# Attention with a 64-key window and a tanh-shrink MLP in one kernel: the first three batches and two chunks issued from one list, batch 0's V transposed on TensorE, weights loaded first

## The chip, the cores and the metric

One core of a Trainium2 chip runs the kernel. Its time is in device microseconds (us). Engines: PE (TensorE; PEld is its weight load), DVE (VectorE), ACT (ScalarE), POOL (GpSimd) and SP (SyncE). DMAs are issued by SP, ACT and POOL. An engine carries out its instructions in the order in which the program issues them.

## The reference

```python
# q, k, v: (batch 8, heads 8, seq 576, head_dim 64), float32
scores = np.matmul(q, k.transpose(0, 1, 3, 2)) / np.sqrt(D)
rel = pos[:, None] - pos[None, :]
mask = (rel >= 0) & (rel < 64)            # each query sees itself and 63 keys before it
attn = softmax(np.where(mask, scores, -1e9))
x = np.matmul(attn, v).transpose(0, 2, 1, 3).reshape(4608, 512)
h = x @ w_in                              # 512 x 2048
g = h - np.tanh(h)
out = g @ w_out                           # 2048 x 512
```

## The kernel before

Work on attention is by pairs of heads: pair g belongs to batch g // 4, four pairs to a batch, 32 in all. A pair's q and k are loaded and cast to bf16, transposed on PE with the heads' dimension on partitions (`tr_heads` for batch 0, `tr_rows` for pairs 4 to 9, `tr` for later ones), and copied from PSUM to `qs` or `qT` and `kT`. The keys are cut into nine windows of 128 (64 of them shared with the window before), the queries into nine blocks of 64. For each window PE makes the scores, ACT the exponential into `PT`, and either DVE multiplies with a 0/1 mask, or PE first writes large negative numbers where a key is hidden (`hides`), so that no mask is needed. PV multiplies with the V windows `vw`, of which there are two buffers, one for even and one for odd batches. V has a column of ones, so that the sum for the norm comes with it; DVE takes the reciprocal and multiplies (`norm`) into `xs`. PE transposes `xs` and a copy brings it to `xT`, the input of the MLP.

V gets to its windows through SBUF: a batch is loaded (`load_v`, `vall`), cast to `vb` (`cast_v`), written to every second window by five DMAs (`windows_v` and `keys_v`, called by `even_windows`), and the other windows are copied from their neighbours by DVE (`odd_windows`, L454 and L456 in the profile).

The MLP goes over nine chunks of 512 tokens. Chunk c has 16 steps h, each of four matmuls of 512 columns (`hp_mm`, L383), a tanh on ACT (L388) and a subtraction on DVE (`g_sub`, L395); and 16 steps y of four matmuls (`yp_mm`, L407), with a copy and a store after each four (`y_out`).

The order is written by hand. Batch 0's attention is issued straight through, then a loop over steps h = 0, 1, ... issues at each step one `OPS` entry (h or y of some chunk) and then whatever `at(h, fn, ...)` has put there. Chunk 0's h stand at the even steps 0 to 30, chunk 1's at 32 to 62, and chunk 0's y at 64 to 79; chunk 2 begins at step 80. Batches 1 and 2 are put between by tables of steps. From batch 3 on, the tables `STEPS`, `LOADS`, `TURNS` and `VALUES` do this.

Most loads stand in POOL's queue, in this order: batch 0's v, pairs 1 to 3, the window DMAs of batch 0, the first half of w_in, batch 1's v, pairs 4 and 5, the second half of w_in, pairs 6 and 7, the windows of batch 1, batch 2's v, pairs 8 to 11, the windows of batch 2, both halves of w_out, batch 3. An instruction in that queue that waits for a semaphore holds up all behind it.

Of the kernel before, what the change touches and what calls it, by code (L numbers as in the profile page):

```python
# [15 lines left out]
def kernel(  # L16
# [62 lines left out]
    stage, rows, whole = {}, {}, {}  # L79

# [98 lines left out]
    def load_w_in(i):  # L179
        nc.gpsimd.dma_start(out=w_in_sb[i], in_=w_in_r[:, :, 1024 * i:1024 * i + 1024])  # L180
# [39 lines left out]
    nc.vector.memset(vw[0][0:64, 0], 0.0)  # L220
# [13 lines left out]

    def tr_heads(g, which, bank, eng):

        src = stage.pop((g, which))
        tp = ps[:, bank, :].bitcast(BF16)[:, 0:E * P].rearrange("c (e p) -> c e p", e=E)
        for e in range(E):
            for h in range(2):  # L240
                nc.tensor.transpose(tp[64 * h:64 * h + 64, e, :], src[:, h, D * e:D * e + D], ident[:P, :P])
        o = qs[g % 2] if which == "q" else kT[g % NK][:, 64:]
        move(eng, o.rearrange("c (p e) -> c p e", e=E), tp.rearrange("c e p -> c p e"))
# [20 lines left out]
    def tr_rows(g, which, bank, eng):  # L264

        src = rows.pop((g, which)).rearrange("p e h d -> p e (h d)")
        tp = ps[:, bank, :].bitcast(BF16)[:, 0:E * P].rearrange("c (e p) -> c e p", e=E)
        for e in range(E):
            nc.tensor.transpose(tp[:, e, :], src[:, e, :], ident[:P, :P])
        o = qs[g % 2] if which == "q" else kT[g % NK][:, 64:]  # L270
        move(eng, o.rearrange("c (p e) -> c p e", e=E), tp.rearrange("c e p -> c p e"))

# [5 lines left out]

    def tile_scores(g, grp, banks, how="hide"):

        j0, n = GROUPS[grp]
        if how == "hide":
            hides(grp, banks)
        for i in range(n):
            j = j0 + i
            for h in range(2):
                r = slice(64 * h, 64 * h + 64)
                nc.tensor.matmul(ps[:, banks[h], 64 * i:64 * i + 64], kT[g % NK][r, 64 * j:64 * j + 128],  # L288
                                 qs[g % 2][r, 64 * j:64 * j + 64], start=how == "mask", stop=how == "mask" or i == n - 1)
        o = PT[g % NPT][:, j0:j0 + n].rearrange("p j (h t) -> p h j t", h=2)  # L290
        nc.scalar.activation(o, pair_of(banks)[:, :, 0:64 * n].rearrange("p h (j t) -> p h j t", t=64),  # L291
                             ACT.Exp, scale=scale)
        if how == "mask":
            p = PT[g % NPT][:, j0:j0 + n].rearrange("p j (h t) -> p (j h) t", h=2)
            nc.vector.tensor_tensor(p, p, mask_sb.unsqueeze(1).to_broadcast([128, 2 * n, 64]), ALU.mult)

    def tile_pv(g, banks):

        b, pr = divmod(g, NP)
        for i in range(NJ + 1):  # L300
            j = min(i, NJ - 1)
            o = 65 * (i % 5)
            for h in range(2):
                nc.tensor.matmul(ps[64 * h:64 * h + 64, banks[i // 5], o:o + 65], PT[g % NPT][:, j, 64 * h:64 * h + 64],
                                 vw[b % 2][:, j, 2 * pr + h, :], start=True, stop=True)
        ov = pair_of(banks)[:, :, 0:325].rearrange("p n (i c) -> p n i c", c=D + 1)
        rc = sm_pool.tile([128, 2, 5, 1], F32, tag="rc2", name="rc2")
        nc.vector.reciprocal(rc, ov[:, :, :, D:D + 1])
        xo = xs[b % 2].rearrange("p (n i) r d -> p n i r d", i=5)
        nc.vector.tensor_tensor(xo[:, :, :, pr, :], ov[:, :, :, 0:D], rc.to_broadcast([128, 2, 5, 64]), ALU.mult)  # L310
# [61 lines left out]
    H0_BANKS = 0, 1, 2, 3, 0, 1, 0, 1, 0, 1, 2, 0, 1, 2, 0, 1  # L372

    def hp_bank(c, m):
        return H0_BANKS[m] if c == 0 else (m + 2) % 3 if c == 1 else m % 2

    def hp_mm(c, ms, split):
# [8 lines left out]
        for m, hp in zip(ms, outs):  # L386
            th = sm_pool.tile([128, TOK], F32, tag="th", name="th")
            nc.scalar.activation(th, hp, ACT.Tanh)  # L388
            HID[c, m] = hp, th

    def g_sub(c, m):
        hp, th = HID.pop((c, m))
        if m == 0:
            gT[c] = g_pool.tile([128, M, TOK], BF16, tag="gT", name="gT")
        nc.vector.tensor_tensor(gT[c][:, m, :], hp, th, ALU.subtract)  # L395

    def yp_bank(c, s):
        if c == 0:
            return s % 2
        return (0, 2)[s % 2] if c == NC - 1 else 2  # L400
# [9 lines left out]
    def y_out(c, s):  # L410
        ysb = sm_pool.tile([128, d_model], F32, tag="ysb", name="ysb")
# [18 lines left out]
    for m in range(M):  # L430
        OPS[2 * m] = "h", 0, m
        OPS[32 + 2 * m] = "h", 1, m
        OPS[64 + m] = "y", 0, m
# [33 lines left out]
    for pr in range(NP):  # L467
        load_v(0, pr)
# [5 lines left out]
    for g in 2, 3:  # L474
        load(g, "k", G)
        load(g, "q", G)
# [212 lines left out]
```

## Time and profile before

| what | value |
|---|---|
| median of 3 runs (lowest to highest) | 334.32 us (333.44 to 335.68) |
| profiled execution: its own time / its span | 334.17 us / 332.4 us |
| PE, DVE, ACT, POOL busy in the span | 315.9, 199.5, 185.1, 110.5 us |
| L383 (h), L407 (y): matmuls of 512 columns | 576 and 560, mean 379 ns each |
| L395 subtraction on DVE, L388 tanh on ACT | mean 689 and 599 ns |
| copies from PSUM of 128x576, ACT / DVE | mean 654 / 754 ns |
| casts of 96x768 (q or k), ACT / DVE / POOL | about 830 / 370 / 830 ns |
| casts of V, 72x1024, DVE / POOL | mean 429 / 1052 ns |
| norm: reciprocal and product of 128x640 on DVE | mean 215 and 824 ns |
| exponential of 128x640 / 128x512 on ACT | mean 702 / 595 ns |
| DMA issue on POOL: load of a pair / window | about 660 / 590 ns |
| w_in's first half: issued / landed | 12.2 / 25.1 us |
| w_out's halves landed | 64.2 and 69.8 us |
| first matmul of chunk 0 / of chunk 2 | 25.1 / 89.5 us |

The profile is of one execution. Its groups of instructions give the mean duration of one; an engine's busy time is the sum of these with overlaps taken once. Matmuls are pipelined, so their mean duration is longer than the distance from one's start to the next's. The chain of waits goes back from the last instruction to what released it, and tells which engine or DMA set the time in each stretch.

### The profile page before, as it was taken

How to read it: one execution, taken by the hardware profiler on the slowest of the kernel's cores; microseconds unless marked ns; L12 is line 12 of the kernel's file. 1: busy time of each engine (PE TensorE's matmuls, PEld its weight loads, DVE VectorE, ACT ScalarE, POOL GpSimd, SP SyncE). 2: the span in 40 equal slices, each digit the busy share in tenths (PEclk: the TensorE clock that was granted, in tenths of full speed). 3: DMA queues.
4: the chain of work that ended last, by engine and by line, in shares of the span. 5: the costliest groups of instructions: out<-in, count | busy, mean ns of one | idle time of the engine just before them, and what ended most of it. 6: DMA issues, size and time to landing. Idle time of an engine off the chain costs nothing.

```text
span 332.4 us, 6239 instructions
## 1 busy us (share of the span) xinstructions
PE 315.9 (95%) x2435; PEld 175.3 (53%) x2435; DVE 199.5 (60%) x342; ACT 185.1 (56%) x339; POOL 110.5 (33%) x163
## 2 busy tenths in 40 slices
PE   6868999899999999999999999999999999999995
PEld 2544565555555655555555555555554444444444
DVE  4578698983257675767676666766665444334400
ACT  3545878872566666656666666555544344444411
POOL 8827597005920845434624493300000000000000
PEclk9599999999999999999999999999999999999999
DMA  8999998993796299384976968978004001000021
GB/s 159 184 173 191 212 161 120 199 190 101 123 198 125 41 163 236 81 118 116 176 133 113 180 142 140 204 126 205 32 34 104 32 34 63 32 34 32 32 97 64
DMA packets 46766, 40.68 MB, mean 122 GB/s; under 512 B 18416, under 2 KB 40048, under 8 KB 46544
## 3 DMA queue, kind: packets, MB, share of 16 engines
q0 software_dynamic: 21344, 20.06, 40.1%
q1 hardware_dynamic: 25184, 19.92, 23.6%
q8 instruction: 19, 0.31, 0.4%
q10 hardware_dynamic: 208, 0.29, 0.3%
q14 instruction: 11, 0.09, 0.1%
HBM read 36.70 MB, written 10.62 MB: 142 GB/s over the span
## 4 chain that ended last, share of the span: by engine, by line
PE 71%; DMA 9%; POOL 7%; DVE 7%; ACT 3%; issue 2%; POOLq 0%; DVEq 0%; ACTq 0%
PE ps L407 34%; PE ps L383 27%; DMA wi<-in_moe_w_in_dram 4%; PE ps L332 3%; DMA kall<-in_k_dram 3%; PE ps L316 3%; DVE xs L343 2%; PE ps L249 2%; DMA vw<-vb 2%; DVE qt L85 2%; POOL qall L96 1%; DVE gT L395 1%; POOL kall L96 1%; POOL vall L143 1%; POOL vb L85 1%
## 5 line engine op out<-in xcount | busy, mean ns | idle before, releaser
L383 PE MATMUL ps<-xT,wi 128*128 128x512 bf16 x576 | 146.8, 379 | 2.9 <-DVE gT L395 1.2
L407 PE MATMUL ps<-w_out_sb,gT 128*128 128x512 bf16 x560 | 140.8, 379 | 0.3 <-ACT ysb L412 0.3
L395 DVE TENSOR_TENSOR gT<-ps,th 128x512 bf16<-128x512 f32 x144 | 98.5, 689 | 68.6 <-ACT th L388 67.2
L388 ACT ACTIVATE th<-ps 128x512 f32<-128x512 f32 x144 | 86.0, 599 | 80.8 <-PE ps L383 77.0
L383 PEld LDWEIGHTS <-wi 128*128 128x128 bf16 x576 | 60.5, 113 | 48.1 <-issue 3.0
L407 PEld LDWEIGHTS <-gT 128*128 128x128 bf16 x560 | 52.2, 98 | 53.0 <-issue 0.8
L318 ACT ACTIVATE pt<-ps 128x384 bf16<-128x384 f32 x66 | 32.3, 489 | 24.1 <-PE ps L316 24.1
L85 POOL COPY vb<-vall 72x1024 bf16<-72x1024 bf16 x24 | 24.7, 1052 | 32.6 <-DMA vall<-in_v_dram 29.8
L343 DVE TENSOR_TENSOR xs<-ps,rc 64x576 bf16<-64x576 f32 x44 | 33.2, 755 | 1.1
L412 ACT ACTIVATE ysb<-ps 128x512 f32<-128x512 f32 x35 | 21.0, 599 | 18.9 <-PE ps L407 18.8
L85 DVE COPY qt<-ps 64x576 bf16<-64x576 bf16 x18 | 13.7, 760 | 24.1 <-ACT qt L83 24.1
L85 POOL COPY qb<-qall 96x768 bf16<-96x768 bf16 x20 | 16.6, 830 | 24.6 <-DVE pt L322 16.4
L332 PEld LDWEIGHTS <-pt 128*128 128x128 bf16 x198 | 16.5, 98 | 15.3 <-DVE pt L322 0.8
L332 PE MATMUL ps<-vw,pt 128*128 128x130 bf16 x198 | 22.0, 220 | 0.4 <-DVE pt L322 0.4
L316 PE MATMUL ps<-qt,kt 128*128 128x128 bf16 x198 | 21.8, 219 | 0.0
L316 PEld LDWEIGHTS <-kt 128*128 128x128 bf16 x198 | 15.4, 98 | 8.9 <-issue 0.3
L85 POOL COPY kb<-kall 96x768 bf16<-96x768 bf16 x20 | 16.6, 828 | 3.0 <-DMA kall<-in_k_dram 3.0
L322 DVE TENSOR_TENSOR pt<-pt,ps 128x1152 bf16<-128x1152 bf16 x22 | 16.4, 745 | 0.8 <-ACT pt L318 0.8
L83 ACT ACTIVATE kt<-ps 128x576 bf16<-128x576 bf16 x22 | 14.4, 654 | 1.6 <-PE ps L249 1.5
L291 ACT ACTIVATE pt<-ps 128x640 bf16<-128x640 f32 (+1 forms) x20 | 12.5, 648 | 2.9 <-PE ps L288 2.9
L96 POOL DMA_DIRECT2D qall<-in_q_dram x15 | 9.9, 662 | 7.9 <-DMA wi<-in_moe_w_in_dram 7.0
L83 ACT ACTIVATE qt<-ps 64x576 bf16<-64x576 bf16 x18 | 11.5, 638 | 1.0 <-PE ps L249 0.9
(79 smaller groups left out, 205.1 us busy)
## 6 DMA issues: line engine op xcount, KB each, us to landing
out_dram<-ysb SPq DMA_DIRECT2D x35, 256.0 KB
vall<-in_v_dram POOLq DMA_DIRECT2D x5, 576.0 KB, 10.7
qall<-in_q_dram POOLq DMA_DIRECT2D x4, 576.0 KB, 11.6
kall<-in_k_dram POOLq DMA_DIRECT2D x4, 576.0 KB, 11.5
kall<-in_k_dram POOLq DMA_DIRECT2D x15, 144.0 KB, 5.4
qall<-in_q_dram POOLq DMA_DIRECT2D x15, 144.0 KB, 5.2
wi<-in_moe_w_in_dram POOLq DMA_DIRECT2D x2, 1024.0 KB, 11.3
w_out_sb<-in_moe_w_out_dram POOLq DMA_DIRECT2D x2, 1024.0 KB, 14.3
```

Source lines behind the costliest of these rows:

```text
L83: nc.scalar.activation(o, i, ACT.Copy)
L85: eng.tensor_copy(o, i)
L96: eng.dma_start(out=t, in_=(q if n == "q" else k)[b, pr::NP].rearrange("h (p e) d -> p h (e d)", e=E))
L316: nc.tensor.matmul(sp[:, i, :], kT[g % NK][:, 64 * j:64 * j + 128], qT[g % NR][:, :, 64 * j:64 * j + 64], start=True, stop=True)
L318: nc.scalar.activation(PT[g % NPT][:, 3 * grp:3 * grp + 3, :], sp, ACT.Exp, scale=scale)
L332: nc.tensor.matmul(ps[:, 5 + grp, 130 * i:130 * i + 130], PT[g % NPT][:, j, :], vw[b % 2][:, j, 2 * pr:2 * pr + 2, :], start=True, stop=True)
L343: nc.vector.tensor_tensor(xo[r, :, :, pr, :], ov[r, :, :, h, 0:D], rc[r].to_broadcast([64, 3, 3, 64]), ALU.mult)
L383: nc.tensor.matmul(hp, w_in_tile(ki, m), chunk_tile(c)[:, :, ki % 2, 64 * (ki // 2):64 * (ki // 2) + 64], start=(ki == 0), stop=(ki == 3))
L388: nc.scalar.activation(th, hp, ACT.Tanh)
L395: nc.vector.tensor_tensor(gT[c][:, m, :], hp, th, ALU.subtract)
L407: nc.tensor.matmul(yp, gT[c][:, m, s * 128:(s + 1) * 128], w_out_sb[:, m, :], start=(m == 0), stop=(m == M - 1))
L412: nc.scalar.activation(ysb, ps[:, yp_bank(c, s), :], ACT.Copy)
```

## The change

- Batch 0's V is loaded like q and k, 96 rows by six (`load_v0`), into a scratch that takes the place of a `gT` buffer. PE transposes it once to have the dimension on partitions (`Tv`), a copy brings it to `vT`, PE transposes each window back (`v_tr`), and a copy brings it to `vw[0]` (`v_copy`). The casts, window DMAs and odd windows of batch 0 are gone.
- w_in (its first half in two pieces) and w_out are loaded right after batch 0, ahead of batches 1 and 2.
- Batches 0, 1 and 2 and chunks 0 and 1 (chunk 1's y apart) are issued from one list, `FIRST`. A table `BANKS` gives each piece its PSUM bank. The list was ordered by a search over a model of the engines. Chunk 0's y now stand between its h and chunk 1's h, and nothing of the MLP stands at steps 64 to 79; the last lines of the list are followed by pair 12's transposes and first scores, and by chunk 2 at step 80.
- Pairs 0 to 3 and 7 are hidden by matmul, the others of these batches masked by DVE. Pairs 10 and 11 have their scores in the form of the earlier pairs.
- Five warming matmuls in batch 0 are gone; four `ysb` buffers in place of three.

How a word of the list is read: `kc.4.A` casts pair 4's k on ACT (`.D`: on DVE). `T` transposes, `C` copies from PSUM, `Vc` casts V. `W` and `X` are the second transpose of V and its copy, `H` hides, `S` scores, `E` exponential, `M` mask, `PV`, `N` norm, `Y` and `Z` the transposes and copies of x (batch, half). `h`, `t`, `u` are an MLP step's matmuls, tanh and subtraction (chunk, step); `y` and `yo` the second matmul and its store. `mv.b` issues batch b's window DMAs and then later loads, `od.b` its odd windows. `a` and `b` are the first five and the last four windows.

```diff
+    def load_v0(pr):
+        nc.gpsimd.dma_start(out=v0[:, pr::NP], in_=v[0, pr::NP].rearrange("h (p e) d -> p h (e d)", e=E))
+        stage[pr, "v"] = v0[:, pr::NP]
...
-    for pr in range(NP):
-        load_v(0, pr)
+    load_v0(0)
     make_ident()
     load(1, "k", G)
     load(1, "q", G)
     make_hide()
+    load_v0(1)
+    load(2, "k", G)
+    load(2, "q", G)
+    load_v0(2)
+    load_v0(3)
+    load(3, "k", G)
+    load(3, "q", G)
     make_seen()
-    for g in 2, 3:
+    load_w_in(0, 0, 512)
+    load_w_in(0, 512, 1024)
+    load_w_in(1)
+    load_w_out(0)
+    load_w_out(1)
+    for pr in range(NP):
+        load_v(1, pr)
+    for g in 4, 5, 6, 7:
         load(g, "k", G)
         load(g, "q", G)
...
+    FIRST = """
+        kc.0.A qc.0.D Ha.0 Tq.0 Tv.0 Tk.0 Cv.0.A Tk.1 Tq.1 Ck.1.A Wa.0 Cq.0.D Ck.0.D Sa.0 Cq.1.D Ea.0 Xa.0.D
+        Hb.0 Tv.1 Sb.0 Eb.0 Ha.1 Cv.1.D Wb.0 Xb.0.D Sa.1 Ea.1 Wa.1 Wb.1 PV.0 Tq.2 Xa.1.A Tk.2 Tv.2 Xb.1.D Hb.1
+        N.0 Sb.1 Cq.2.A Ha.2 Tv.3 Cv.2.A Wa.2 Ck.2.D Eb.1 Cv.3.A Sa.2 Xa.2.D Tk.3 Ck.3.D Hb.2 Sb.2 Ea.2 Wb.3
+        Eb.2 Xb.3.D Tq.3 Wb.2 PV.1 Cq.3.D Wa.3 Ha.3 N.1 Xb.2.A Sa.3 Hb.3 Sb.3 PV.2 Ea.3 Xa.3.D Eb.3 PV.3 Ya.0.0
+        Yb.0.0 N.2 N.3 Za.0.0.A Zb.0.0.A Ya.0.1 Yb.0.1 Za.0.1.A Zb.0.1.D h.0.0 h.0.1 t.0.0 h.0.2 h.0.3 h.0.4
...
+        u.0.11 h.0.15 t.0.13 t.0.14 u.0.12 t.0.15 u.0.13 Vc.6.A Vc.5.A kc.4.A y.0 u.0.14 u.0.15 y.1 Vc.7.D
+        qc.4.D Vc.4.D y.2 y.3 y.4 y.5 yo.0 Tq.4 Tk.4 y.6 Ck.4.A Cq.4.D Sb.4 qc.5.D kc.5.D Eb.4 Sa.4 Tq.5 qc.6.D
+        y.7 kc.6.D Cq.5.D Ea.4 Tk.5 yo.1 Ck.5.A qc.7.D Tk.6 Tq.6 Cq.6.A y.8 Ck.6.D mv.1 kc.7.D Sa.5 Sa.6 Tk.7
+        Ea.5 Ea.6 y.9 Tq.7 Mb.4 Ck.7.A Ma.4 Sb.6 Sb.5 od.1 y.10 Cq.7.D y.11 Ha.7 Eb.6 Ma.6 Eb.5 Mb.5 Vc.8.A Sa.7
+        yo.2 Hb.7 Sb.7 Ea.7 Mb.6 Vc.10.D Eb.7 PV.4 Ma.5 N.4 PV.6 kc.8.D qc.8.A N.6 y.12 PV.7 Vc.11.A PV.5 N.5
+        y.13 qc.9.A Vc.9.A Tq.8 N.7 Tk.8 kc.9.A Tq.9 y.14 Yb.1.1 Ck.8.D Cq.9.A mv.2 Tk.9 Ya.1.0 Ya.1.1 Zb.1.1.D
+        Cq.8.A Ck.9.A kc.10.D Yb.1.0 Za.1.0.A y.15 Sa.8 yo.3 Sb.8 Zb.1.0.D Ea.8 Za.1.1.D h.1.0 qc.10.D Eb.8 od.2
+        h.1.1 Mb.8 Sb.9 Sa.9 t.1.0 h.1.2 t.1.1 u.1.0 Ma.8 h.1.3 Ea.9 u.1.1 Eb.9 Tk.10 qc.11.A Ma.9 PV.8 Mb.9 N.8
...
+        Zb.2.0.A N.10 PV.11 u.1.9 t.1.10 u.1.10 h.1.12 t.1.11 t.1.12 h.1.13 N.11 u.1.11 u.1.12 Ya.2.1 h.1.14
+        t.1.13 u.1.13 Yb.2.1 Za.2.1.A Zb.2.1.D t.1.14 h.1.15 t.1.15 u.1.14 u.1.15
+    """.split()
+    HIDE = (0, 1, 2, 3, 7)
...
+    def v_tr(c, g):
+        j0, n = half(c)
+        tp = v_psum(c, g)
+        for i in range(n):
+            nc.tensor.transpose(tp[:, i].rearrange("p h d -> p (h d)"), vT[:, g, 64 * (j0 + i):64 * (j0 + i) + 128], ident)
+
+    def v_copy(c, g, eng):
+        j0, n = half(c)
+        move(eng, vw[0][:, j0:j0 + n, 2 * g:2 * g + 2, 0:D], v_psum(c, g))
...
+    def first_moves(b):
+        even_windows(b, G, G, G, G, G)
+        if b == 1:
+            for pr in range(NP):
+                load_v(2, pr)
+            for g in 8, 9:
+                load(g, "k", G)
+                load(g, "q", G)
+        else:
+            for g in 10, 11:
+                load(g, "k", G)
+                load(g, "q", G)
...
     warm(9)
...
+    for t in FIRST[:FIRST.index("h.0.3")]:
+        first(t)
     see()
     copy_mask()
...
+    for t in FIRST[FIRST.index("h.0.3"):]:
+        first(t)
+    load_all(3, "q")
+    load_all(3, "k")
+    load_v_all(3)
+    at(67, lambda: nc.gpsimd.tensor_copy(tick, gT[1][0:1, 9, 0:1]))
...
-    STEPS = {2: (0, 0, 49, 57), 3: (72, 79, 86, 93), 4: (100, 107, 114, 121), 5: (128, 135, 142, 149)}
+    STEPS = {3: (74, 80, 87, 93), 4: (100, 107, 114, 121), 5: (128, 135, 142, 149)}
...
-    for h in range(32 * NC + 64):
-        op = OPS.get(h)
+    for h in range(64, 32 * NC + 64):
+        op = OPS.get(h) if h > 79 else None
```

## The prediction

> **What bounds the kernel now.** I read the page first (busy shares, clock, costliest groups), then busy time by stage, then the chain of waits in order of time, then the timeline of the start. The page:
>
> ```profile
> span 332.4 us, 6239 instructions
> PEclk9599999999999999999999999999999999999999
> L383 PE MATMUL ps<-xT,wi 128*128 128x512 bf16 x576 | 146.8, 379 | 2.9 <-DVE gT L395 1.2
> L395 DVE TENSOR_TENSOR gT<-ps,th 128x512 bf16<-128x512 f32 x144 | 98.5, 689 | 68.6 <-ACT th L388 67.2
> L388 ACT ACTIVATE th<-ps 128x512 f32<-128x512 f32 x144 | 86.0, 599 | 80.8 <-PE ps L383 77.0
> ```
>
> PE is the bound over the span, but its clock was granted at half in the second slice. The stages, cut at the first matmul of chunk 0 (25.1) and of chunk 2 (89.5):
>
> ```profile
> 8.00:16.00 8.00, 6.36 (x126) 4.60 (x119) 4.41 (x9) 4.38 (x8) 7.02 (x12) 0.50 1.10 189
> 16.00:25.10 9.10, 6.28 (x129) 3.81 (x125) 7.31 (x15) 4.25 (x10) 2.36 (x4) 0.88 1.10 171
> 25.10:89.50 64.40, 60.94 (x625) 35.11 (x626) 47.20 (x90) 43.87 (x82) 36.65 (x53) 1.00 0.96 162
> 89.50:332.40 242.90, 237.45 (x1526) 129.67 (x1523) 137.30 (x217) 129.86 (x239) 57.84 (x80) 1.00 0.52 107
> ```
>
> Columns: length, PE, PEld, DVE, ACT, POOL busy, clock, DMA share. A busy PE here counts the whole latency of pipelined matmuls (mean 379 ns), so I price PE by spacing, which the chain shows (start, length, what):
>
> ```profile
> 12.16 12.91 DMA wi<-in_moe_w_in_dram
> 26.79 10.24 DMA kall<-in_k_dram
> 51.68 6.05 DMA vw<-vb
> 58.12 0.70 DVE vw L454
> 63.31 0.51 PE ps L304 x20
> 65.04 0.26 PE ps L249 x6
> 76.31 3.45 PE ps L407 x16
> ```
>
> Up to 58 us DMA carries the chain; after it PE does. A 512-column matmul costs 0.216 us (3.45/16), 20 PV matmuls 0.51, 6 transposes 0.26. At half clock:
>
> ```profile
> 13.14 0.69 PE L241 MATMUL ps<-ident,qall 96*64 96x96 bf16 x12
> 13.87 0.69 PE L241 MATMUL ps<-ident,kall 96*64 96x96 bf16 x12
> 16.06 1.12 PE L276 MATMUL ps<-hide,ident 128*128 128x320 bf16 x4
> 17.11 0.66 PE L288 MATMUL ps<-qs,kt 64*128 64x64 bf16 x18
> 17.71 0.61 PE L233 MATMUL ps<-qt 128*128 128x512 bf16 x1
> ```
>
> By starts: 12 transposes 0.73, a pair's hides 1.05, its 18 scores 0.60. One more view prices a lone load on POOL's queue (188 to 208 us):
>
> ```profile
> qall<-in_q_dram POOLq DMA_DIRECT2D x3, 144.0 KB, 4.8
> kall<-in_k_dram POOLq DMA_DIRECT2D x3, 144.0 KB, 4.9
> ```
>
> **What the Trainium skill says.** "TensorE: Matmul & The Clock Gate", Part 1, says that the default clock is half and that a window of some 3.4 us of sustained work releases it; its Part 4 says that transposes don't count as such work. The trace agrees: from 11.9 to 14.6 us nearly all is transposes and the clock stays 0.50; it rises in the stretch with hides, scores and a 512-column matmul. The same page (architectural detail in Part 1) has ACT and DVE strictly first in, first out; the reading of order below rests on it, and no line here shows otherwise. "DMA: Bandwidth & Descriptors", the anatomy of a SWDGE DMA, puts about 2.0 us fixed on one DMA and says that the issuing sequencer does the waiting. The trace has 4.8 us for 144 KB, and I use that.
>
> **Batch 0, up to the first matmul of chunk 0.** Removed: four V casts on DVE, five window DMAs, two odd-window copies (0.86 and 0.70 us) after which all PV waited, 2 pairs' masks, five warming matmuls. Added: 48 transposes (four times 12), 36 transposes of 128 columns, eight copies (some 0.6 to 0.75 us each), hides for two pairs more. PE at half clock: twelve groups of 12 transposes 8.8, hides 4 x 1.05 = 4.2, scores 4 x 0.60 = 2.4, second V transposes 36 x 0.11 (twice 0.22/4, the warm price) = 4.0, PV 2.1, x transposes 2.0: 23.5 us, from about 5.9. DVE has some 15 us from 5.2, spread over the stage, where before four norms (1.04 each) stood in a row at its end. The last of the ten loads lands near 14.5 in both. If the clock comes at about 18, as before, 12.3 us are done by then and the remaining 11.2 shrink to 6.2: PE ends at 24.4, and with the last copy of 0.6 chunk 0 starts at 25.0. If it comes at 11.4, the chain of waits gives 23.2; if transposes keep it down through the stage, 27. I take 25.0 (before: 25.1): the V path trades DMA waits for PE work at half clock.
>
> **Weights first.** The two w_out loads took 6.4 and 5.6 us from landing to landing and now stand ahead of batches 1 and 2, so w_out lands near 37 instead of 70; that lets y of chunk 0 fill the middle. Batch 1's last q lands near 45 by 0.7 us a load, when it is wanted; this hides. Batch 2's V windows landed at 57.7 before; now about 12 us of weights stand in front.
>
> **Chunk 0 to h.1.0.** PE: 32 groups of four matmuls x 0.864 = 27.6; 12 transpose sets x 0.26 = 3.1; scores of pairs 4 to 8 2.7; one hide 0.7; PV of 4 to 7 2.0; x transposes 1.0. Sum 37.1. From y.6 on ACT has 18.6, PE 17.7, DVE 17.1: three engines in step, each in its fixed order. I add 2.2 for waits (at least the 0.9 by which ACT exceeds PE; the old stage took 64.4 for some 57 of PE at these spacings).
>
> **The new stall.** On DVE `kc.10` stands ahead of `Zb.1.0` and `Za.1.1`, without which `h.1.0` cannot start. Pair 10's load is queued on POOL behind the five window DMAs of batch 2, and those wait for `Vc.9` on ACT. From the end of pair 7's scores: ACT does Eb.7 and four casts (0.83 + 1.04 + 0.83 + 1.04) and ends Vc.9 at +4.6. Five issues of about 0.55 and then 4.8 to land: k of pair 10 is there at +12.3; its cast 0.37 and the copies 0.57 and, for the second half, 0.42 (hidden behind the first matmuls). h.1.0 can start at +13.3. PE has PV, y.12 to y.15 and transposes, 8.1 us, until it stands there; DVE is free at +7.0. Stall: about 5, taken as 4.8. From below: 0, if the load lands in 2 us and PE is late anyway; from above 6.5, with the windows at the 7.2 us which the DMA view of 83 to 87 gives them. Behind `kc.10` wait q's cast, od.2 and all of DVE; behind h.1.0 all of chunk 1.
>
> **h.1.0 to the end of the list.** DVE: 16 subtractions x 0.689 = 11.0; masks of four pairs 3.6; four norms 4.2; od.2 1.5; cast 0.4; K copy 0.75; x copies 1.0. Sum 22.4, against PE 19.6 and ACT 19.2. PE ends some 2 us ahead of DVE's last subtraction, and coupling takes about that back: 22.0.
>
> **The hand-over.** Before, steps 64 to 79 laid y of chunk 0 between pair 12's transposes and scores. Now nothing lies there: after h.1.15 come tr q, tr k and scores(12, 0), then chunk 2. Scores wait for both halves of qT: ACT's tanh (0.1 + 0.6), its copy 0.64, then DVE's subtraction and copy 0.76, so 2.35 us after h.1.15; with the three scores 2.5. PE has 0.5 of transposes for it: a hole of 1.85 us that has no cover.
>
> **Sum.** 25.0 + 37.1 + 2.2 + 4.8 + 22.0 + 2.5 = 93.6 for the first matmul of chunk 2. Before: 89.5, with three scores and six transposes of pairs 12 and 13 (0.4) already behind it. So +4.5 us. What follows is the same, and PE waited there 1.3 us in all; batch 3's windows, on POOL after u.1.9, land near 8 us into chunk 2, and PV of its last windows asks near 9: taken as nothing. The profiled execution took 334.17 us (span 332.4, 1.8 around it), 0.15 below the median of the runs, 334.32. 334.17 + 4.5 = 338.7.
>
> **Rivals.** *The stages fill, and it is faster* (the other side): one mechanism, that the load of pair 10 is no later than PE. It decides if k lands within some 3 us less than priced and clock comes early. Then 23.2 + 37.1 + 1.5 + 20.6 (PE with 1.0 of waits) + 2.9 = 85.3, 4.2 less: 330.0. For it: 7 us of old waits in 25 to 89 can go, and DMA was the chain till 58; against it: three loads in a row at 4.8. *Cold and late*: transposes hold the clock at half until 25 (27 for the start, +2), batch 3's windows land 2 us after PV asks: 342.5. For it: 84 more transposes; against it: the hides of two pairs more do count as work. A change within 1% needs the stall at half its price; that lies in the likeliest case's own spread, 335 to 342.
>
> **Chances.** Likeliest 0.58, faster 0.22, cold and late 0.20. One per cent, 3.3 us, is about what a measurement can tell. Of the likeliest, two thirds lie above 337.7 and one third within 1%; of the faster, four fifths below 331.0; of the cold case nearly all above. Slower 0.57, same 0.25, faster 0.18. The range runs from 330.5 to 343.5: it holds the likeliest, most of the cold case and the upper part of the faster one.
>
> **What would show it.** Chunk 0 at 25 (23.2 or 27 with the clock); kb of pair 10 on DVE waiting for its DMA for about 5 us, and PE idle ahead of h.1.0; DVE without a gap from there on; PE idle for about 1.9 us ahead of scores(12, 0), released by DVE qT; chunk 2 near 93.6. It is wrong if kb waits for under 1 us, or if chunk 2 starts before 89.

## The result and the profile after

The changed kernel takes 351.07 us (median of 4 runs, 349.41 to 353.89), the kernel before 334.39 beside it: ratio 1.0505, 95% interval 1.0417 to 1.0592. It is slower, as forecast, but by 16.7 us and not by 4.5; 351.07 lies above my range, which ended at 343.5. The profiled execution took 349.41 us, the shortest of the four. One run of e9 below (353.73 us) lies more than 1.5% above the fastest of its kernel and is left out of its median and ratio.

The page, by the same lines as before (span, clock in 40 slices, first matmul, subtraction, tanh):

```profile
span 347.7 us, 6488 instructions
...
PEclk9976999899999999999999999999999999999999
...
L338 PE MATMUL ps<-xT,wi 128*128 128x512 bf16 x576 | 146.6, 382 | 3.3 <-DVE xT L93 2.3
...
L355 DVE TENSOR_TENSOR gT<-ps,th 128x512 bf16<-128x512 f32 x144 | 98.2, 690 | 68.9 <-ACT th L348 66.5
L348 ACT ACTIVATE th<-ps 128x512 f32<-128x512 f32 x144 | 85.7, 598 | 81.2 <-PE ps L338 77.4
```

The instructions of the MLP cost what they did. What is new stands in the clock: it is low in the third and fourth slice (21.5 to 31.7 us) and not in the second. Busy time by stage, cut at the first matmul of chunk 0 (28.9), of chunk 1 (76.1) and of chunk 2 (102.8):

```profile
8.00:16.00 8.00, 5.44 (x142) 4.09 (x140) 3.96 (x8) 4.58 (x8) 7.06 (x12) 1.00 1.22 182
16.00:28.90 12.90, 8.32 (x161) 6.25 (x159) 6.41 (x13) 5.40 (x10) 1.97 (x3) 0.71 1.12 214
28.90:76.10 47.20, 40.32 (x393) 21.58 (x394) 27.02 (x54) 29.54 (x46) 19.45 (x31) 0.93 0.81 132
76.10:102.76 26.66, 21.17 (x256) 12.35 (x256) 21.65 (x42) 18.31 (x33) 7.56 (x11) 1.00 0.54 87
102.76:347.70 244.94, 237.91 (x1534) 129.99 (x1531) 137.67 (x217) 130.61 (x239) 62.18 (x88) 1.00 0.53 106
```

Every stage is longer than forecast: the start by 3.9 (25.0), chunk 0 to chunk 1 by 3.1 (44.1 with the stall), the rest of the list with the hand-over by 2.2 (24.5), and all that follows by 2.0 (242.9 before). Up to chunk 2 no engine is full in any of them (PE, the busiest, 40.3 of 47.2 us between chunk 0 and chunk 1). What PE waited for (line, what it waited for, total us, times, longest):

```profile
PE ps L563 <- ACT pt L546: 2.6, 2, 1.6
...
PE ps L338 <- DVE xT L93: 2.3, 2, 1.5
PE ps L511 <- ACT pt L546: 2.3, 3, 1.3
PE ps L541 <- ACT pt L546: 2.3, 2, 1.2
PE ps L525 <- ACT pt L546: 2.1, 2, 1.8
PE ps L276 <- DVE qt L93: 1.7, 1, 1.7
...
PE ps L288 <- DMA vw<-vb: 1.6, 2, 1.3
```

Three of these I had named: the wait of chunk 1 (L338), the hand-over (L276), and PV of batch 3 (L288). Of the others, PV (L563) may well wait for an exponential (L546), whose result it reads. But transposes of q and k (L511) and of V (L525) wait for one too, and they don't read its result. They would have to wait only if they wrote into a bank that it still reads; the next section looks at which banks these are.

### The profile page after: what moved, and what is told of

The parts are those of the page before. It is cut to its first block, busy times and chain, and to the rows that moved or that the text cites. A ratio compares the mean times of both kernels' runs of the same rounds, so it can differ in the third digit from the quotient of the medians.

```text
span 347.7 us, 6488 instructions
## 1 busy us (share of the span) xinstructions
PE 319.1 (92%) x2554; PEld 177.4 (51%) x2554; DVE 201.4 (58%) x349; ACT 191.8 (55%) x339; POOL 104.9 (30%) x159
## 4 chain that ended last, share of the span: by engine, by line
PE 68%; issue 8%; DMA 8%; DVE 7%; POOL 5%; ACT 4%; POOLq 0%; DVEq 0%; ACTq 0%
PE ps L338 28%; PE ps L367 28%; DMA vw<-vb 5%; DMA qall<-in_q_dram 3%; PE ps L288 3%; PE ps L276 2%; DVE xs L299 2%; PE ps L251 2%; ACT pt L546 1%; PE ps L563 1%; POOL vb L93 1%; DVE gT L355 1%; DVE qt L93 1%; POOL vw L158 1%; PE ps L382 1%
## 5 line engine op out<-in xcount | busy, mean ns | idle before, releaser
L338 PE MATMUL ps<-xT,wi 128*128 128x512 bf16 x576 | 146.6, 382 | 3.3 <-DVE xT L93 2.3
L338 PEld LDWEIGHTS <-wi 128*128 128x128 bf16 x576 | 61.0, 114 | 51.8 <-issue 5.5
L278 ACT ACTIVATE pt<-ps 128x384 bf16<-128x384 f32 x60 | 29.3, 489 | 22.9 <-PE ps L276 22.9
L299 DVE TENSOR_TENSOR xs<-ps,rc 64x576 bf16<-64x576 f32 x40 | 30.2, 755 | 1.0
L93 POOL COPY vb<-vall 72x1024 bf16<-72x1024 bf16 x20 | 20.7, 1054 | 28.5 <-DMA vall<-in_v_dram 28.5
L93 DVE COPY qt<-ps 64x576 bf16<-64x576 bf16 x16 | 12.2, 760 | 20.9 <-ACT qt L91 20.8
L288 PEld LDWEIGHTS <-pt 128*128 128x128 bf16 x180 | 15.2, 98 | 15.2 <-issue 1.5
L546 ACT ACTIVATE pt<-ps 128x640 bf16<-128x640 f32 (+1 forms) x24 | 15.1, 650 | 13.4 <-PE ps L338 3.3
L288 PE MATMUL ps<-vw,pt 128*128 128x130 bf16 x180 | 20.3, 220 | 1.6 <-DMA vw<-vb 1.6
L276 PE MATMUL ps<-qt,kt 128*128 128x128 bf16 x180 | 19.8, 219 | 1.7 <-DVE qt L93 1.7
L93 POOL COPY qb<-qall 96x768 bf16<-96x768 bf16 x20 | 16.7, 834 | 8.1 <-DMA qall<-in_q_dram 8.1
L276 PEld LDWEIGHTS <-kt 128*128 128x128 bf16 x180 | 13.9, 98 | 8.7 <-ACT kt L91 1.4
L282 DVE TENSOR_TENSOR pt<-pt,ps 128x1152 bf16<-128x1152 bf16 x20 | 14.9, 744 | 0.0
L104 POOL DMA_DIRECT2D kall<-in_k_dram x15 | 9.6, 640 | 7.0 <-DMA w_out_sb<-in_moe_w_out_dram 4.5
```

The source lines that it names most:

```text
L93: eng.tensor_copy(o, i)
L104: eng.dma_start(out=t, in_=(q if n == "q" else k)[b, pr::NP].rearrange("h (p e) d -> p h (e d)", e=E))
L276: nc.tensor.matmul(sp[:, i, :], kT[g % NK][:, 64 * j:64 * j + 128], qT[g % NR][:, :, 64 * j:64 * j + 64], start=True, stop=True)
L278: nc.scalar.activation(PT[g % NPT][:, 3 * grp:3 * grp + 3, :], sp, ACT.Exp, scale=scale)
L288: nc.tensor.matmul(ps[:, 5 + grp, 130 * i:130 * i + 130], PT[g % NPT][:, j, :], vw[b % 2][:, j, 2 * pr:2 * pr + 2, :], start=True, stop=True)
L299: nc.vector.tensor_tensor(xo[r, :, :, pr, :], ov[r, :, :, h, 0:D], rc[r].to_broadcast([64, 3, 3, 64]), ALU.mult)
```

## The experiments

Landmarks of the profiled executions and the times, in us (first matmul of chunk 0, 1 and 2, span, median of the runs, ratio to the kernel before with its interval). The column "0 to 1" is the time from chunk 0's first matmul to chunk 1's.

| kernel | chunk 0 | chunk 1 | chunk 2 | span | 0 to 1 | median | ratio |
|---|---|---|---|---|---|---|---|
| before | 25.1 | | 89.5 | 332.4 | | 334.4 | |
| changed | 28.9 | 76.1 | 102.8 | 347.7 | 47.2 | 351.07 | 1.0505 [1.042, 1.059] |
| e1 neighbouring pairs | 23.4 | 71.7 | 97.1 | 343.2 | 48.3 | 343.86 | 1.0297 [1.026, 1.034] |
| e2 bank by bank | 22.9 | 71.5 | 97.0 | 344.0 | 48.6 | 342.83 | 1.0249 [1.020, 1.030] |
| e3 before, pairs apart | 30.8 | | 94.4 | 337.5 | | 339.08 | 1.0142 [1.011, 1.018] |
| e4 = e1, cast later | 23.5 | 62.7 | 95.3 | 341.4 | 39.3 | 342.33 | 1.0244 [1.020, 1.028] |
| e5 = e1, loads earlier | 23.5 | 62.9 | 92.1 | 339.2 | 39.4 | 340.74 | 1.0185 [1.015, 1.022] |
| e6 = e1, stall filled | 23.2 | 69.1 | 92.3 | 338.5 | 46.0 | 340.55 | 1.0204 [1.016, 1.025] |
| e7 = e1, POOL held less | 22.4 | 69.4 | 93.8 | 336.2 | 47.1 | 338.76 | 1.0145 [1.011, 1.018] |
| e8 = e1, all supply edits | 22.7 | 63.1 | 87.0 | 329.3 | 40.4 | 330.56 | 0.9881 [0.985, 0.991] |
| e9 changed, supply edits | | | | | | 348.43 | 1.0435 [1.036, 1.051] |
| e10 = e8, w_out later | 23.9 | 64.9 | 89.7 | 335.8 | 41.0 | 337.51 | 1.0101 [1.004, 1.016] |
| e11 = e8, hand-over | 23.2 | 61.6 | 83.6 | 331.6 | 38.4 | 331.12 | 0.9890 [0.983, 0.996] |
| e12 = e8, V by DMA | 33.3 | 74.4 | 97.6 | 339.5 | 41.1 | 341.31 | 1.0189 [1.014, 1.024] |

### Waits between instructions that share no bank (e1, e2, e3)

The theory. An exponential reads the scores of two heads, and a norm two halves of PV, each half in a bank of its own. Both take them as one slice:

```python
def pair_of(banks):
    a, b = banks
    return ps[:, a:b + 1:b - a]
```

For banks (0, 7) this is `ps[:, 0:8:7]`. All of PSUM is one tile, `ps`, of eight banks here, and the waits of the program are made as if such a slice covered all the banks from 0 to 7. In the kernel before every pair was (0,1), (2,3), (4,5) or (6,7), where that makes no difference. In the table of the changed kernel 27 of 36 pairs lie apart. I compared, for each wait in the program, the banks and tiles of the two instructions: 49 waits in the changed kernel are between two that share none, and none in the kernel before. Here is such a chain in the trace of the changed kernel (start, length, what, [idle before <- releaser]; lines of POOL, PEld and others left out):

```profile
8.26 0.70 ACT L546 ACTIVATE pt<-ps 128x640 bf16<-128x640 f32 x1 [0.72 <-PE ps L541]
...
9.01 0.38 PE L269 MATMUL ps<-hide,ident 128*128 128x256 bf16 x2 [0.80 <-ACT pt L546]
...
10.66 0.76 DVE L93 COPY scratch<-ps 128x576 bf16<-128x576 bf16 x1 [1.88 <-ACT pt L546]
...
11.85 0.70 ACT L546 ACTIVATE pt<-ps 128x640 bf16<-128x640 f32 x1 [1.22 <-DVE vw L93]
...
12.60 0.66 PE L525 MATMUL ps<-ident,scratch 128*128 128x128 bf16 x9 [1.76 <-ACT pt L546]
```

By the table: the exponential at 8.26 reads banks 1 and 6, and the hides at 9.01 write 2 and 5. The copy of V at 10.66 reads bank 3 and waits for the next exponential, which reads 2 and 5. The exponential at 11.85 reads 0 and 7 and waits for a copy out of bank 6, though both only read PSUM; the transposes at 12.60 write banks 4 and 5 and wait for this exponential. Four such waits follow one on the other, on PE, DVE and ACT in turn. The same instructions in e1:

```profile
8.28 0.55 PE L269 MATMUL ps<-hide,ident 128*128 128x256 bf16 x2
...
9.25 0.76 DVE L93 COPY scratch<-ps 128x576 bf16<-128x576 bf16 x1 [0.34 <-PE ps L507]
...
10.21 0.68 PE L525 MATMUL ps<-ident,scratch 128*128 128x128 bf16 x9
...
10.32 0.70 ACT L546 ACTIVATE pt<-ps 128x640 bf16<-128x640 f32 x1 [0.26 <-PE ps L541]
```

None of the four waits is left, and the transposes start 2.39 us earlier (10.21 for 12.60).

**e1** changes nothing but the table of banks, for example:

```diff
-        k0:2 q0:3 v0:0 wa0:0 wb0:6 Sa0:16 Sb0:25 PV0:23 k1:4 q1:7 v1:3 wa1:4 wb1:5 Sa1:07 Sb1:45 PV1:26 k2:7
+        Sa0:01 q0:4 v0:6 k0:3 k1:2 q1:7 wa0:5 Sb0:67 v1:4 Sa1:23 wb0:1 wa1:0 wb1:7 PV0:56 q2:4 k2:0 v2:1 Sb1:23
```

> The changed kernel with one table altered: every pair of PSUM banks that one exponential or one norm reads now lies in neighbouring banks; the list, its order, the engines and the loads are untouched. Theory F (false waits): an instruction that reads two banks that lie apart is tracked over all the banks between them, so that 49 instructions in the changed kernel wait for one with which they share neither bank nor tile. Then this table alone takes back most of what my forecast missed (351.1 measured against 338.7 forecast): chunk 0 starts near 25 to 26.5 (28.9 before), chunk 2 near 93 to 97 (102.8), total 337 to 345. Rival P (the waits I priced are larger than priced: kc.10, hand-over, clock): banks don't matter, total within 1% of 351. Rival C (the clock alone): batch 0 as slow as in the changed kernel, chunk 0 at 28 or later, the middle unchanged.

Measured: 343.86, 7.2 less. Chunk 0 starts at 23.4, earlier than I forecast and 5.5 earlier than in the changed kernel; chunk 2 at 97.1. (The two profiled executions differ by only 4.5 us of span: the changed kernel's is the shortest of its four runs, e1's the longest.) The theory stands so far; but the table also gives many single pieces another bank, and e2 tells whether that matters. What is left to my forecast, 5.2 us, must have other causes.

**e2** keeps the table and takes the pair out of the instruction:

```diff
-        nc.scalar.activation(PT[g % NPT][:, j0:j0 + n].rearrange("p j (h t) -> p h j t", h=2),
-                             pairs_psum(f"S{c}{g}")[:, :, 0:64 * n].rearrange("p h (j t) -> p h j t", t=64),
-                             ACT.Exp, scale=scale)
+        for h in range(2):
+            nc.scalar.activation(PT[g % NPT][:, j0:j0 + n, 64 * h:64 * h + 64],
+                                 ps[:, BANKS[f"S{c}{g}"][h], 0:64 * n].rearrange("p (j t) -> p j t", t=64),
+                                 ACT.Exp, scale=scale)
```

(the norm likewise).

> The changed kernel with its own bank table, but each exponential and each norm of the list is done bank by bank, in two instructions of half the size, so that no instruction spans two banks. Theory F: the false waits go as with neighbouring pairs, against some 24 x 0.2 us more on ACT and 12 x 0.5 us more on DVE, of which in the DVE-bound second part some 2 us show: 338 to 348. Rival P: nothing is gained and the added instructions cost, 352 to 357. Both this and the run with neighbouring banks gain if it is the span of banks; only the other gains if it is which bank is reused when.

Measured: 342.83, chunk 0 at 22.9, though ACT and DVE have more to do. So it isn't which bank is taken when; it is that one instruction spans two distant banks. (An exponential of half the size can also start when its half of the scores is there; how much of the gain that is was not separated.)

**e3** goes the other way, in the kernel before:

```diff
-    tile_scores(0, 0, (0, 1))
+    tile_scores(0, 0, (0, 7))
...
-    tile_pv(0, (6, 7))
+    tile_pv(0, (1, 6))
```

and so for all of batch 0's pairs in banks 1 and 7.

> The kernel before with banks 1 and 7 exchanged in batch 0 alone, so that pairs which lay side by side (0,1) and (6,7) lie apart (0,7) and (1,6); nothing else changes. Theory F: 11 instructions now wait for one with no bank in common; batch 0 gets longer by 0.5 to 3 us (chunk 0 at 25.6 to 28), total 334.8 to 337.5. Rival P: no change, within 0.3%.

Measured: 339.08, 4.6 more than before, and chunk 0 5.7 later; more than I expected. Hides and scores wait for an exponential with which they share no bank:

```profile
9.46 0.59 PE L276 MATMUL ps<-hide,ident 128*128 128x256 bf16 x2 [0.79 <-ACT pt L291]
...
14.30 0.40 PE L288 MATMUL ps<-qs,kt 64*128 64x64 bf16 x8 [1.27 <-ACT pt L291]
...
21.58 0.76 PE L304 MATMUL ps<-vw,pt 128*64 128x65 bf16 x20
```

PE works at half clock all the while: the trace's record of the clock begins only at 30.9, with the full clock, but 20 PV matmuls take 0.76 here and 0.51 at full clock. Not all of that comes from the exchange. The first transposes, at 6.3 us in both kernels and ahead of anything that was edited, take 0.69 here and took 0.45 in the kernel before. So the exchange cost the kernel 1.4% in all, the clock has a part in it, and how large a part was not separated. That the false waits arise is shown by the waits themselves: in the kernel before, no hide or score of batch 0 waits for an exponential.

### The stall ahead of chunk 1 (e4, e5, e6)

I had forecast that the cast of pair 10's k, standing ahead of the copies of x, costs chunk 1 4.8 us. In the changed kernel the cast waited 2.46 and PE 1.51:

```profile
67.54 0.60 POOL L173 DMA_DIRECT2D vw<-vb  x1 [10.09 <-ACT vb L91]
...
75.42 0.35 DVE L93 COPY kb<-kall 96x768 bf16<-96x768 bf16 x1 [2.46 <-DMA kall<-in_k_dram]
...
76.10 1.98 PE L338 MATMUL ps<-xT,wi 128*128 128x512 bf16 x8 [1.51 <-DVE xT L93]
```

That is the chain as I had written it down (ACT's last cast of V releases POOL, the windows go ahead, then the load), but PE was so late by the other waits that little of it shows. With these gone, in e1:

```profile
71.03 0.36 DVE L93 COPY kb<-kall 96x768 bf16<-96x768 bf16 x1 [8.79 <-DMA kall<-in_k_dram]
...
71.70 2.72 PE L338 MATMUL ps<-xT,wi 128*128 128x512 bf16 x6 [7.44 <-DVE xT L93]
```

**e4**, in the list:

```diff
-        Cq.8.A Ck.9.A kc.10.D Yb.1.0 Za.1.0.A y.15 Sa.8 yo.3 Sb.8 Zb.1.0.D Ea.8 Za.1.1.D h.1.0 qc.10.D Eb.8 od.2
+        Cq.8.A Ck.9.A Yb.1.0 Za.1.0.A y.15 Sa.8 yo.3 Sb.8 Zb.1.0.D Ea.8 Za.1.1.D h.1.0 kc.10.D qc.10.D Eb.8 od.2
```

> The version with neighbouring bank pairs, and in the list the cast of pair 10's k (kc.10, on DVE) is moved behind the copies of x that the first matmul of chunk 1 needs. My forecast held that this cast waits for its load and costs chunk 1's start 4.8 us. If so: 3 to 5 us less than the version with neighbouring pairs alone. Rival (the delay is given back, since DVE bounds the rest of the list and its work is only moved): 0 to 1.5 us less. If with neighbouring pairs the load is in time: no difference.

Measured: chunk 1 starts at 62.7, 9.0 earlier, but chunk 2 only 1.8 earlier, and the median is 1.5 lower. The gain came and went:

```profile
PE ps L563 <- DVE gT L355: 4.0, 1, 4.0
PE ps L511 <- DVE kb L93: 2.8, 1, 2.8
```

The second line is pair 10's transposes, which now wait for the cast; the first is PV of pair 8, which waits on DVE for the odd windows and the masks behind them. The rival had the right size, but not the reason that it gave (DVE's own work): one late supply had hidden the next, and with it the clock went to half for 10.2 us again (69.0 to 79.2).

**e5** removes the cause instead, in `first_moves`:

```diff
-            for g in 8, 9:
+            for g in 8, 9, 10, 11:
                 load(g, "k", G)
                 load(g, "q", G)
-        else:
-            for g in 10, 11:
-                load(g, "k", G)
-                load(g, "q", G)
```

> The version with neighbouring bank pairs, with the loads of pairs 10 and 11 issued right behind those of 8 and 9, ahead of the window DMAs of batch 2; the list is untouched. In the version with neighbouring pairs the cast of pair 10's k waited 8.8 us for its load and PE 7.4 us ahead of chunk 1, while the clock fell to half for 10 us. Theory S (the order of POOL's queue sets it): the cast waits for under 1 us, chunk 1 starts near 64 (71.7 before); the next wait is od.2 for batch 2's windows, some 3 us ahead of PV.8; chunk 2 starts near 92 to 94 (97.1), total 339 to 341.5 (343.9). Rival (DVE sets the rest of the list, the gain is given back): chunk 2 at 95.5 or later, total above 342.

Measured: chunk 1 at 62.9, chunk 2 at 92.1, 340.74, all in the interval of the theory. What is left is batch 2's windows:

```profile
68.45 0.70 DVE L413 COPY vw<-vw 64x2080 bf16<-64x2080 bf16 x1 [5.60 <-DMA vw<-vb]
...
71.98 0.76 PE L563 MATMUL ps<-vw,pt 128*64 128x65 bf16 x20 [4.69 <-DVE gT L355]
```

The trace names the last release (a subtraction); DVE was held up by the windows long before.

**e6** asks what the half clock costs, by 30 matmuls on zeros in the stall:

```diff
+            if (c, m) == (1, 0):
+                warm(30, hp_bank(1, 0))
             hp_mm(c, (m,), m == 0)
```

> The version with neighbouring bank pairs, with 30 added matmuls of 512 columns on zeros just ahead of chunk 1's first matmul, in the bank that this matmul overwrites: they fill 6.5 us of the 7.4 us for which PE waited there, and change no dependence. Theory K (the half clock after the stall costs by itself): the clock stays full between 66 and 77, and chunk 2 starts 1.5 to 4 us earlier (93 to 95.5), total 340 to 342.5. Rival (DVE and windows bound that stretch, so the clock costs nothing): total within 1 us of 343.9; if the added matmuls come too late, slower by up to 1.

```profile
61.72 6.65 PE L245 MATMUL ps<-qt 128*128 128x512 bf16 x30
...
68.46 0.36 DVE L93 COPY kb<-kall 96x768 bf16<-96x768 bf16 x1 [8.30 <-DMA kall<-in_k_dram]
...
69.14 1.99 PE L338 MATMUL ps<-xT,wi 128*128 128x512 bf16 x8 [0.77 <-DVE xT L93]
```

The cast waits as long as before (8.30), the clock stays full from 7.5 to 96.2, and chunk 1 to chunk 2 takes 23.1 us and not 25.4: the half clock of 10.2 us cost 2.2. The median is 3.3 lower, inside the interval of theory K. (Chunk 1 itself starts 2.6 earlier in this execution, since pair 10's k landed earlier; no edit reaches that far back, so that I don't count it. How the 3.3 divides between the two is therefore not shown, and the 2.2 rests on one execution of each kernel.)

### Batch 3's windows and the whole supply (e7, e8, e9)

**e7**, one number:

```diff
-    at(67, lambda: nc.gpsimd.tensor_copy(tick, gT[1][0:1, 9, 0:1]))
+    at(67, lambda: nc.gpsimd.tensor_copy(tick, gT[1][0:1, 2, 0:1]))
```

> The version with neighbouring bank pairs, with the instruction on POOL that holds batch 3's casts and window DMAs back until chunk 1's subtraction 9 waiting for subtraction 2 instead. I had taken the windows of batch 3 as late by nothing; measured, chunk 2 on took 246.1 us of span against 242.9 in the kernel before, with PE waiting 2.1 us for POOL's cast of q ahead of pair 13's transposes and the clock at half for 3.4 us. Theory W (POOL is late there): the wait of 2.1 goes, from chunk 2 to the end near 243.5, total 340.5 to 342.5. Rival: POOL's casts now run beside DVE's bounding stretch and slow it; chunk 2 later by 0.5 to 2 us, total 342.5 to 344.5.

The stretch from chunk 2 on, in e1 and then in e7 (columns as in the table of stages: length, PE, PEld, DVE, ACT, POOL busy, clock, DMA share):

```profile
97.07:343.20 246.13, 239.28 (x1534) 130.59 (x1531) 137.71 (x217) 130.98 (x239) 63.66 (x91) 0.99 0.54 106
```

```profile
93.77:336.20 242.43, 237.66 (x1534) 130.20 (x1531) 137.97 (x217) 130.60 (x239) 59.04 (x83) 1.00 0.52 104
```

3.7 us less, where I expected 2.6; the wait for POOL's cast is gone. POOL's earlier casts did not visibly slow DVE's stretch: 24.3 us from chunk 1 to chunk 2 against 25.4, with a mean clock of 0.94 for 0.90. The median fell by 5.1, below both expectations. The other part lies ahead of chunk 2: chunk 0 starts 1.0 earlier in the profiled execution, which no edit reaches, and the half clock after the stall lasts 6.8 and not 10.2 us.

**e8** puts the supply edits together: e1, the cast later (e4), the loads earlier (e5), the hold shorter (e7), and two casts of V ahead of those of q, so that POOL can issue batch 2's windows 5 us earlier (56.1 for 61.3):

```diff
-        yo.2 Hb.7 Sb.7 Ea.7 Mb.6 Vc.10.D Eb.7 PV.4 Ma.5 N.4 PV.6 kc.8.D qc.8.A N.6 y.12 PV.7 Vc.11.A PV.5 N.5
-        y.13 qc.9.A Vc.9.A Tq.8 N.7 Tk.8 kc.9.A Tq.9 y.14 Yb.1.1 Ck.8.D Cq.9.A mv.2 Tk.9 Ya.1.0 Ya.1.1 Zb.1.1.D
+        yo.2 Hb.7 Sb.7 Ea.7 Mb.6 Vc.10.D Eb.7 PV.4 Ma.5 N.4 PV.6 Vc.9.A Vc.11.A kc.8.D qc.8.A N.6 y.12 PV.7 PV.5 N.5
+        y.13 qc.9.A Tq.8 N.7 Tk.8 kc.9.A Tq.9 y.14 Yb.1.1 Ck.8.D Cq.9.A mv.2 Tk.9 Ya.1.0 Ya.1.1 Zb.1.1.D
```

> Everything that supplies batches 2 and 3 in one: neighbouring bank pairs, pair 10's k cast behind the copies of x, the loads of pairs 10 and 11 ahead of batch 2's windows, two of batch 2's V casts ahead of the casts of q on ACT (so that the windows are issued near 56 and not 61), and the hold on POOL ended at subtraction 2. If the stages as I priced them (37.1 plus 2.2 to chunk 1, 22.0 to the end of the list, 2.5 for the hand-over) hold without the stall: chunk 1 at 62.5, chunk 2 at 87, total 330 to 333, below the kernel before. If DVE and the supply still collide: chunk 2 at 89 to 92, total 334 to 338. If the bank pairs alone were the cause: near 343.

```profile
22.70:63.11 40.41, 38.38 (x396) 21.14 (x394) 27.71 (x57) 28.82 (x46) 20.08 (x32) 0.97 1.10 194
63.11:87.02 23.91, 21.15 (x261) 12.71 (x256) 20.93 (x41) 19.30 (x35) 10.94 (x16) 1.00 0.74 118
87.02:329.30 242.28, 237.50 (x1534) 129.96 (x1531) 137.54 (x217) 130.61 (x239) 58.89 (x83) 1.00 0.52 105
```

Measured: 330.56, 1.2% faster than the kernel before. Chunk 0 to chunk 1 takes 40.4, where PE's sum and the waits gave 39.3; chunk 1 to chunk 2 23.9, where DVE's 22.0 and the hand-over's 2.5 gave 24.5. PE is busy in 38.4 of the first 40.4. So the list that the search made is a good one with three words of it moved, but not with its table of banks and its order on POOL.

**e9** applies the same supply edits to the changed kernel with its own table of banks.

> The changed kernel with its own bank table (pairs apart), and with all the supply edits of the run before (pair 10's cast later, loads of 10 and 11 ahead of the windows, two V casts earlier, the hold on POOL ended at subtraction 2). Neighbouring pairs alone were worth 7.2 us, the supply edits on top of them 13.3. If the two causes add up: 351.1 - 13.3 = 337.8. Theory O (they overlap: in the changed kernel the false waits make PE late, so that the loads are nearly in time, 1.5 us of idle ahead of chunk 1): the supply edits are worth 3 to 6 us here, total 345 to 348.

Measured: 348.43 (347.75 to 351.91). That is 2.6 below 351.07, but the intervals of the two ratios overlap, so no gain is shown, and theory O's 3 us are not excluded either. What is excluded is the sum of the two causes: 337.8 would be 10 us below the fastest run, where the same edits gained 13.3 on e1. The likely reason is theory O's: as long as the false waits make PE late, the supply is nearly in time (PE waited 1.5 ahead of chunk 1), and little is gained by making it earlier. The trace of e9 can't confirm it: in that execution the clock was half from 9.8 to 40.5 and chunk 0 started at 34.7, although its batch 0 is the changed kernel's.

### Single parts of the change, from the fast version (e10, e11, e12)

**e10** loads w_out behind batch 1 again.

```diff
-    load_w_out(0)
-    load_w_out(1)
     for pr in range(NP):
         load_v(1, pr)
     for g in 4, 5, 6, 7:
         load(g, "k", G)
         load(g, "q", G)
+    load_w_out(0)
+    load_w_out(1)
```

> The fast version (neighbouring pairs and supply edits, 330.6) with w_out's two loads moved behind those of batch 1, undoing that part of the change. w_out's halves then land near 38 and 44 by the spacing of landings; PE comes to y of chunk 0 at 38, so that it waits 2 to 5 us there, and batch 1's early landing is of no use, since the list has nothing of it on PE before y. Total 332 to 336. Rival (w_out ahead of batch 1 is what makes the middle late): 328 to 330.

```profile
PE ps L367 <- DMA w_out_sb<-in_moe_w_out_dram: 2.8, 1, 2.8
PE ps L288 <- DMA vw<-vb: 1.9, 1, 1.9
```

Measured: 337.51, 7.0 slower, beyond the 2 to 5 that I expected. The wait at y of chunk 0 is there with 2.8; chunk 2 starts 2.7 later. The rest of the span, 3.8, comes after: PV of batch 3 waits, and the clock is half for 3.4 us there. "Weights first" is needed by this list.

**e11** brings pair 12's transposes into the list.

```diff
-        t.1.13 u.1.13 Yb.2.1 Za.2.1.A Zb.2.1.D t.1.14 h.1.15 t.1.15 u.1.14 u.1.15
+        t.1.13 u.1.13 Yb.2.1 Za.2.1.A Zb.2.1.D t.1.14 zt h.1.15 t.1.15 u.1.14 u.1.15
...
+    def first_zt():
+        tr(12, "q", 5, A, V)
+        tr(12, "k", 0, A)
```

(and `zc` behind `u.1.3`, with batch 3's loads, the hold and pair 12's casts.)

> The fast version with pair 12's casts (POOL) and transposes (PE, in banks that are free then) moved into the list, the transposes ahead of chunk 1's last four matmuls. I forecast a hole of 1.85 us ahead of scores(12, 0); measured 1.7 in every kernel with the list. If it is what it seems: the wait of 1.7 is gone or under 0.3, chunk 2 starts 1 to 1.7 us earlier, total 329 to 329.8. Rival (DVE bounds the end of the list, and the copy moved ahead of its last subtractions makes them later): gain under 0.5.

```profile
PE ps L288 <- DMA vw<-vb: 2.4, 1, 2.4
...
PE ps L251 <- POOL qb L93: 1.4, 1, 1.4
...
PE ps L276 <- DVE qt L93: 0.4, 1, 0.4
```

The wait falls from 1.7 to 0.4, and from chunk 1 to chunk 2 it takes 22.0 and not 23.9 (chunk 1 was 1.5 earlier already). Then PV of batch 3 waits 2.4 for its windows, a transpose 1.4 for POOL, and the clock falls for 3.4 us: from chunk 2 on it takes 248.0 for 242.3. (This execution, 333.33 us, is the longest of four.) The total is 331.12, no different from e8's 330.56. The gain turned into a new wait, though not in the way the rival had it: DVE was not what took it back, batch 3's supply was.

**e12** brings batch 0's V to its windows by DMA again, with casts on DVE; PV and norms stand behind the last scores, and the banks are neighbours.

```diff
-    load_v0(0)
+    for pr in range(NP):
+        load_v(0, pr)
...
+                     w0=lambda: [windows_v(0, j, Y) for j in (0, 4, 2, 8, 6)])
```

> The fast version with batch 0's V as in the kernel before: loaded 72 rows by eight, cast by DVE, brought to its windows by five DMAs (here all on SP's queue) and two odd-window copies, all PV after the last scores; no transposes of V. I forecast the V transposes as worth nothing (chunk 0 at 25.0 against 25.1). If so: chunk 0 within 0.7 us of the 22.7 of the fast version, total within 1 of 330.6. If PE has no work while the windows come and the clock falls, as in the kernel before: chunk 0 at 24.5 to 26, total 332 to 334.

```profile
25.96 0.70 DVE L411 COPY vw<-vw 64x2080 bf16<-64x2080 bf16 x1 [6.75 <-DMA vw<-vb]
```

```profile
27.44 1.26 PE L556 MATMUL ps<-vw,pt 128*64 128x65 bf16 x38 [6.66 <-DVE vw L413]
```

Both expectations were too low: chunk 0 starts at 33.3, 10.6 later, and the total is 10.8 higher. The windows, issued from 12.7 to 15.5, were there at 25.9: they share the DMA engines with w_in and w_out, whose loads were already in the queues (w_in's second half landed at 27.2). In the kernel before the windows stood ahead of the weights and were in at 17.2. So this part's worth hangs on the other: with weights first, V must not need a DMA. How much of it is the later issue and how much the sharing was not separated: the first window was issued 3.1 us later than in the kernel before, and the last was in 8.7 later. The clock has a part in it as well. In this execution it is on record as full only from 37.3, and twelve transposes at 7.3 us took 0.69, where e8, at full clock from 5.0, took 0.45:

```profile
7.30 0.69 PE L500 MATMUL ps<-ident,qb 96*64 96x96 bf16 x12
```

```profile
5.81 0.45 PE L507 MATMUL ps<-ident,qb 96*64 96x96 bf16 x12
```

## Why the prediction missed

- **Batch 0 (25.0 forecast, 28.9 measured).** Two terms were wrong, with opposite signs. I priced PE at half clock up to about 18 us. The clock was full from 4.4 to 21.5; twelve transposes took 0.45 and not 0.69. (The step from 11.2 us of work to 6.2 at full clock wasn't a halving either, which gives 5.6.) And the sum had no term for the waits between distant banks: 5.5 us (28.9 against 23.4 in e1), the fall of the clock at 21.5 included. I had read `BANKS` as a table of places and not asked what a slice over two of them makes other instructions wait for. This is the step that failed, and the largest: all such waits of the list together are 7.2 of the 12.4 us by which the time exceeded the forecast. None of the signs that I had set for being wrong could show it: kb did wait for more than 1 us, and chunk 2 did not start before 89.
- **Chunk 0 to chunk 1 (37.1 plus 2.2).** Right once the stall is out: 39.3 in e4, 39.4 in e5, 40.4 in e8; the 2.2 for waits was a guess that held. In the changed kernel 47.2, of which 1.5 is the stall.
- **The stall (4.8).** The mechanism was right, its size wrong both ways: 1.5 behind the false waits, 7.4 without them. In the changed kernel the load of pair 10's k behind five windows took 4.9 us (70.5 to 75.4), as good as the 4.8 that I had priced, and PE was late; in e1 it took 6.8 (64.2 to 71.0). And I priced a stall at its length. By e4 its end alone is worth 1.5, since batch 2's windows are late next; I had noted that 12 us of weights now stood ahead of these, and gave that no term. By e6 the clock that falls after the stall costs 2.2 more.
- **Chunk 1 to chunk 2 (22.0 plus 2.5).** Right without false waits and stall: 23.9 in e8, 23.1 in e6. In the changed kernel 26.7. The hole of the hand-over was forecast as 1.85 and measured as 1.7, released by DVE's qt as written.
- **Weights first.** w_out landed at 29.4 and 34.3 (forecast: near 37), batch 1's last q at 42.9 (forecast: near 45). That it hides is right; by e10 the order is worth 7.0 to the fast version.
- **Batch 3's windows ("taken as nothing").** From chunk 2 on it is 2.0 longer than before in the changed kernel and 3.2 in e1; e7 gets 3.7 back. I had the last one landing 8 us into chunk 2; it landed 8.9 into it (111.6), and PV waited 1.6, inside the 2 that I had set as the upper end. The term should have been that end and not zero: POOL was held to 94.9 by subtraction 9 and issued the windows from 100.9 on.
- **The rivals.** "The stages fill" gave 330.0 and asked for pair 10's load to be no later than PE. When the runs made it so, together with neighbouring banks and earlier windows, the time was 330.6. That the totals agree so closely is in part luck: chunk 2 started at 87.0 in e8 and at 85.3 in the rival's sum. "Cold and late" had the right direction; its late windows came (1.6 us for the 2 that it gave them), its cold start did not: the clock was full from 4.4 on, among transposes.

For e1 the balance against the forecast's own stages is: start -1.6; chunk 0 to chunk 1 +4.2 (the stall 7.4 for 4.8 is 2.6 of it); chunk 1 to chunk 2 +0.9, with the half clock's 2.2 in it; from chunk 2 on +3.2. The sum, 6.7, is what the spans differ by (343.2 against 93.6 + 242.9).

## What to carry to other kernels

When a kernel's buffers are placed by a table, look for instructions that span two places with a gap, and count the waits between instructions that have no buffer in common: there should be none. In the profile they show as an engine that waits for an instruction whose result it doesn't use and whose banks it doesn't write. Price a stall not by its length but by what is late next, and move all of a queue's late supplies together. Here single ones gave 1.5, 3.1 and 5.1 us, all of them with two casts moved as well 13.3, and at most little of it showed while another cause held the consumer back.

## What was not expected of the hardware

The Trainium skill, "TensorE: Matmul & The Clock Gate", Part 4, says that transposes don't count as PE being busy, for the clock, in the way that other matmuls do. Here the clock was full for 17.1 us in batch 0 (4.4 to 21.5) with more transposes than in the kernel before, with hides and scores between them. It fell after 3.4 us (18.1 to 21.5) in which PE was busy for 1.85. In e3, with fewer transposes, PE ran at half clock through the whole stage. So the number of transposes did not decide it alone. That gaps on PE did is a reading and not shown: no run changed the gaps alone, and in the traced execution of e9 the changed kernel's batch 0 ran at half clock from 9.8 on.

The same page's Part 1 puts the return to half clock at an idle window of some 3.4 us. The traces agree in the unit: the low stretches were 3.41, 6.83 or 10.24 us long, and 30.7 in e9. But PE need not idle for a whole one: a longest wait of 1.24 came ahead of the 10.2 us in the changed kernel, one of 2.4 ahead of 3.4 us in e11, one of 7.4 around the start of the 10.2 in e1. Thirty matmuls on zeros in place of that wait kept the clock up (e6).

Window DMAs from SBUF to SBUF that took some 5 us in the kernel before (issued from 9.6, all landed by 17.2) took 10 and more beside the loads of the weights, issued from SP's queue (e12).
